# First weight matrix loaded in one transfer per quarter, its first tile swapped while converting, under a new order of all steps

## The chip, the core and the metric

The kernel runs on one core of one Trainium2 chip. The metric is the device time of one execution in microseconds (us), as the median of several executions; lower is better. A profile is one execution taken by the hardware profiler, with times counted from its first instruction. The engines are PE (matmuls; PEld is its loading of stationary operands), DVE, ACT and POOL (which convert, scale, mask and copy), and SP, which here only issues transfers. SPq is SP's queue of such issues.

## What is computed

Attention over 4 batches, 8 heads, 768 positions of width 64, then a two-layer network over the 3072 rows that come out of it. Heads 0, 2 and 6 are causal over all keys; in the other five each query sees the first four keys and the last 64. Inputs and output are 32-bit; the matmuls take bf16.

```
scores = q @ k^T / 8
keep   = causal                                    (heads 0, 2, 6)
         causal and (key < 4 or query - key < 64)  (other heads)
a      = softmax(scores where keep)
x      = (a @ v) with the heads side by side       [3072, 512]
h      = x @ w_in                                  [3072, 2048]
out    = (h / (1 + exp(-beta * h))) @ w_out        [3072, 512]
```


## The kernel before

**Units.** The work is cut into eight units n = 0..7: batch n // 2 and half n % 2 of its 768 positions, 384 rows each. A unit goes through these steps, named here by a letter, the unit and an index:

- loads of q, k (`load_qk` for units 0 to 2, four pairs of heads each; `load_block` for units 3 to 7, two blocks of three transfers) and of v (`load_v`), each followed by a conversion to bf16 (`cast_...`), mostly on POOL;
- T: transposes of q and k on PE (units 0 to 2); units 3 to 7 use a transposing transfer instead (`turn_block`, three per unit, written QK<-c in the profile);
- S: score matmuls, followed by E, the exponential on ACT, and M, the masks on DVE;
- sum: the row sums on PE. In units 0 and 1 their reciprocals stay on chip (rec and hl on DVE, sb on PE); from unit 2 on they go out and come back spread over the partitions by transfers (`sums_turn`, `spread_w`, `spread_r`, tile R);
- O: a @ v on PE, then the normalisation into xT, 512 x 384 in bf16;
- h.n.s for s = 0..15 (`mm1`, line 899): four matmuls that make 128 of the 2048 columns of h; then t.n.s (`swish_a`, ACT) and g.n.s (`swish_b`, DVE);
- m.n.1 to m.n.48 (`mm2`, line 916): the 48 matmuls of the second layer, 16 for each of three blocks of 128 rows; the sums are copied out (`out_copy`) and stored (`out_store`).

**Weights.** Both weight matrices are loaded once, in quarters, each into one of three staging buffers `wf` of 1 MB that the q, k and v blocks of later units also use (`RINGS`, line 217). A quarter of w_in covers 512 columns and four tiles of 128 rows. In the first tile the two halves of 64 rows must change places, because the pair of heads that makes the first 128 rows of xT lies the other way round (`XT`). `load_w_in` (line 472) does that while loading: one transfer of 768 KB for tiles 1 to 3 and two of 128 KB for the halves of tile 0. Then four conversions of 128 x 512 on POOL (`cast_w_in`, line 489) write `w_in_sb`. Quarter s serves h.n.4s to h.n.4s+3. A quarter of w_out is one transfer of 1 MB and four conversions; conversion i serves second-layer step i in each block of 16.

**The order.** Nothing is ordered by the loops. Every step is put in a list (`plan.add`) with its engine or a choice of engines, a price, what it needs and which buffers it takes. `SEQUENCE` (line 37) is a written-out permutation of that list and `CHOICE` (line 92) picks the engine where there is a choice. `_Plan.run` (line 137) goes through the list in that order, gives each step a start by the prices, and sorts by it; the code is then emitted in that order, and each engine runs its own steps strictly in the order of emission. So an engine whose next step must wait holds back everything behind it, SP's issues included. The prices are only used for that sorting, and for one more thing: in the first two units, wherever PE is planned to be idle before a step, `fill` (line 513) puts in matmuls with no use of their result, one per 0.14 us of planned gap.

**Transfers in flight.** The transfers use eight semaphores in turn, and an issue waits until the earlier transfer on its semaphore has landed, so that at most eight are in flight.

In every profile line the source line is that of a helper (L112 before), so groups are told apart by tile names.

Of the kernel before, what the change touches and what calls it, by code (L numbers as in the profile page):

```python
# [25 lines left out]
RD = 2  # L26
# [11 lines left out]
    474, 475, 6, 466, 4, 8, 14, 468, 12, 478, 467, 20, 10, 0, 2, 16, 5, 469, 473, 9, 7, 33, 471, 29, 77, 34,  # L38
    31, 13, 89, 32, 15, 30, 37, 477, 18, 50, 38, 39, 51, 11, 79, 40, 85, 1, 56, 43, 52, 3, 490, 35, 25, 41,
    27, 36, 26, 57, 42, 28, 17, 44, 45, 21, 47, 78, 91, 48, 53, 80, 97, 54, 59, 86, 102, 480, 23, 100, 24,  # L40
    101, 58, 103, 60, 49, 116, 19, 46, 117, 118, 55, 61, 22, 120, 62, 463, 121, 485, 479, 492, 119, 122, 73,
    493, 90, 63, 92, 491, 123, 114, 75, 64, 74, 81, 115, 112, 76, 83, 125, 481, 65, 87, 126, 67, 113, 69, 484,
    66, 134, 482, 71, 68, 135, 483, 137, 108, 70, 500, 139, 109, 72, 488, 520, 82, 93, 524, 138, 84, 104, 464,
    140, 127, 489, 95, 465, 528, 521, 494, 105, 522, 529, 486, 532, 536, 495, 136, 525, 487, 530, 106, 142,
    526, 88, 533, 143, 534, 502, 540, 107, 98, 110, 503, 547, 505, 111, 94, 541, 128, 548, 131, 501, 542, 551,
    132, 124, 555, 141, 129, 96, 549, 556, 559, 133, 159, 130, 560, 504, 557, 99, 144, 552, 510, 499, 553,
    155, 145, 497, 537, 498, 538, 157, 156, 496, 146, 515, 507, 563, 158, 509, 561, 570, 508, 564, 160, 147,
    523, 571, 148, 506, 527, 565, 572, 163, 531, 167, 153, 149, 151, 511, 535, 171, 150, 512, 161, 152, 574,
    513, 165, 154, 578, 575, 514, 173, 582, 579, 576, 169, 580, 586, 583, 218, 518, 592, 584, 476, 587, 517,
    596, 588, 516, 470, 597, 519, 539, 593, 598, 162, 543, 546, 594, 168, 222, 550, 172, 554, 174, 170, 184,  # L50
    185, 558, 544, 164, 166, 562, 190, 186, 188, 191, 193, 175, 189, 566, 187, 600, 221, 196, 569, 573, 192,
    601, 577, 194, 581, 567, 219, 181, 602, 198, 220, 604, 199, 197, 182, 224, 608, 201, 200, 585, 609, 195,
    227, 225, 203, 605, 610, 589, 223, 204, 606, 228, 612, 202, 206, 590, 205, 619, 613, 207, 226, 176, 208,
    620, 177, 623, 621, 209, 591, 614, 210, 627, 631, 229, 628, 635, 632, 629, 237, 633, 636, 235, 642, 568,
    624, 637, 239, 646, 238, 650, 211, 647, 625, 240, 212, 178, 472, 269, 595, 651, 648, 241, 599, 652, 242,
    654, 179, 643, 249, 655, 603, 236, 252, 644, 213, 658, 250, 253, 607, 656, 659, 244, 660, 611, 247, 271,
    615, 245, 618, 622, 243, 251, 616, 254, 248, 273, 626, 180, 255, 630, 257, 183, 634, 246, 256, 638, 258,
    272, 641, 639, 259, 270, 617, 645, 260, 649, 261, 214, 216, 231, 215, 280, 653, 232, 657, 217, 275, 661,
    664, 662, 274, 278, 668, 665, 276, 672, 669, 666, 277, 676, 262, 673, 230, 233, 670, 674, 677, 279, 678,
    680, 684, 681, 691, 682, 263, 685, 695, 326, 692, 686, 699, 693, 696, 703, 700, 697, 707, 663, 701, 714,  # L60
    704, 708, 718, 289, 705, 709, 715, 722, 726, 716, 264, 723, 234, 667, 727, 290, 281, 671, 724, 293, 282,
    728, 675, 719, 283, 291, 730, 720, 679, 731, 292, 315, 284, 295, 732, 683, 296, 687, 298, 690, 694, 688,
    300, 297, 698, 319, 303, 294, 327, 301, 302, 702, 304, 328, 706, 265, 299, 329, 267, 266, 689, 305, 330,
    545, 268, 710, 306, 713, 717, 307, 721, 370, 725, 317, 736, 729, 737, 321, 740, 738, 316, 711, 733, 324,
    741, 744, 318, 734, 748, 320, 742, 745, 752, 322, 749, 746, 323, 756, 308, 753, 750, 763, 754, 325, 757,
    767, 764, 758, 771, 640, 765, 768, 775, 309, 772, 366, 769, 779, 773, 776, 786, 777, 790, 787, 286, 780,
    788, 334, 332, 285, 739, 335, 287, 794, 336, 781, 743, 795, 310, 337, 791, 796, 747, 338, 792, 798, 339,
    369, 802, 799, 346, 367, 803, 800, 751, 349, 373, 368, 804, 755, 347, 376, 759, 762, 288, 760, 341, 372,
    766, 344, 333, 375, 770, 340, 342, 371, 774, 343, 374, 351, 350, 345, 778, 354, 348, 377, 782, 352, 785,
    311, 353, 355, 313, 312, 356, 789, 357, 314, 793, 358, 386, 797, 331, 387, 735, 801, 390, 712, 412, 808,  # L70
    388, 812, 809, 378, 392, 813, 810, 805, 395, 379, 814, 816, 391, 783, 359, 380, 820, 806, 817, 360, 824,
    416, 821, 818, 828, 822, 825, 835, 393, 826, 839, 396, 829, 836, 397, 830, 843, 389, 837, 840, 847, 361,
    844, 841, 851, 394, 848, 845, 415, 858, 849, 862, 852, 413, 859, 866, 853, 414, 860, 870, 863, 417, 864,
    400, 811, 419, 871, 815, 398, 418, 872, 422, 819, 867, 823, 868, 421, 399, 874, 401, 381, 827, 875, 420,
    402, 876, 362, 403, 404, 364, 363, 761, 831, 834, 423, 365, 838, 842, 429, 846, 880, 832, 850, 405, 881,
    431, 406, 882, 884, 807, 432, 382, 383, 888, 885, 892, 889, 886, 384, 854, 424, 890, 893, 857, 433, 861,
    426, 833, 855, 865, 407, 894, 869, 385, 896, 900, 425, 897, 434, 898, 907, 436, 911, 901, 784, 908, 873,
    902, 856, 877, 909, 912, 915, 878, 913, 919, 430, 916, 879, 427, 923, 920, 917, 930, 924, 921, 934, 435,
    925, 938, 931, 942, 932, 939, 408, 943, 940, 410, 409, 935, 883, 887, 411, 946, 944, 443, 936, 947, 891,
    895, 446, 447, 948, 952, 444, 953, 438, 954, 899, 441, 903, 439, 956, 442, 445, 906, 957, 448, 437, 958,  # L80
    910, 449, 914, 451, 450, 440, 918, 904, 960, 452, 453, 922, 454, 961, 926, 455, 964, 962, 968, 965, 905,
    929, 969, 933, 966, 937, 970, 428, 941, 945, 927, 949, 456, 972, 928, 950, 457, 979, 973, 983, 980, 974,
    987, 981, 984, 991, 988, 985, 995, 989, 992, 1002, 996, 993, 458, 1006, 997, 1003, 1010, 1007, 1004, 1014,
    1008, 1018, 1015, 955, 1011, 1016, 1012, 1019, 951, 1020, 959, 963, 967, 971, 975, 978, 976, 982, 977,
    986, 990, 994, 998, 1001, 999, 1005, 459, 460, 1000, 461, 1009, 462, 1013, 1017, 1021, 1024, 1022, 1028,
    1025, 1023, 1032, 1029, 1026, 1036, 1030, 1033, 1040, 1037, 1034, 1044, 1038, 1041, 1051, 1045, 1042,
    1055, 1046, 1052, 1059, 1056, 1053, 1063, 1057, 1060, 1067, 1064, 1061, 1073, 1065, 1068, 1076, 1069,
    1079, 1077, 1027, 1080, 1078, 1031, 1081, 1074, 1082, 1075, 1085, 1083, 1035, 1086, 1084, 1039, 1087,
    1043, 1047, 1048, 1050, 1054, 1049, 1058, 1062, 1066, 1070, 1088, 1071, 1089, 1072, 1092, 1090, 1091,
    1093, 1094, 1095,  # L90
]
CHOICE = (
    "aaddagaggdgdadadadaadddaddaaddgaagggdaaadaadaaaddaaaddaggdgdgaggadggdgdaadaadaaadaadadadddadddaaa"
# [95 lines left out]
def kernel(  # L189
# [15 lines left out]
    B, H, S, D = q.shape  # L205
    d_model, d_ff = moe_w_in.shape
    FO = d_ff // 128
    NP = len(PAIRS)
# [263 lines left out]
    def load_w_in(s):  # L472
        f = stg.tile([128, 2048], F32, name="wf", bufs=RINGS["wf"]).rearrange("p (a n) -> p a n", a=NP)

        def rows(r, n, tiles):
            return bass.AP(moe_w_in.tensor, moe_w_in.offset + r * d_ff + s * 2 * FS,
                           [[d_ff, n], [128 * d_ff, tiles], [1, 2 * FS]])
        sp.dma_start(out=f[:, 1:4, :], in_=rows(128, 128, 3))
        sp.dma_start(out=f[0:D, 0:1, :], in_=rows(D, D, 1))
        sp.dma_start(out=f[D:128, 0:1, :], in_=rows(0, D, 1))  # L480
        wst["i", s] = f
# [7 lines left out]
    def cast_w_in(s, i, eng):  # L489
        c = slice(i % 2 * 128, (i % 2 + 1) * 128)  # L490
        cast(eng, w_in_sb[2 * s + i // 2][:, :, c], wst["i", s][:, :, i * 128:(i + 1) * 128])
# [473 lines left out]
    def attention(n, early):  # L965
# [3 lines left out]
        for pi in range(NP if n < TD else 0):  # L969
            for nm in ("q2", "k2"):  # L970
                e = "act" if n == 0 and nm == "k2" else "sp"
                add(e, 0.47, lambda pi=pi, nm=nm, e=e: load_qk(x, pi, nm, ENG[e]), dma=0.63,
                    gives=[("f", n, pi, nm)], take=[(nm + "f", (n, pi), 1)])
                e = ("pool", "dve", "act") if early else ("pool",)
                add(e, [{"dve": 0.3, "pool": 0.47, "act": 0.41}[i] for i in e],
# [265 lines left out]
```

## Time and profile before

| | us |
|---|---|
| median of three executions | 240.97 (240.55 to 242.45) |
| span of the profiled execution, first to last instruction | 238.9 |
| median less span | 2.1 |
| PE busy, all stages | 224.3 |
| DVE busy / ACT busy / POOL busy | 153.9 / 141.9 / 90.8 |
| first h.0.s matmul starts | 27.98 |
| last matmul of the program ends | 235.8 |

The page cuts the span into 40 slices of 6 us and gives busy shares in tenths. For the stages the answer by windows is of more use: in it each row is a stretch (from:to, its length), then for PE, PEld, DVE, ACT and POOL the busy time and the number of instructions, then the TensorE clock that was granted (1.00 is full), the busy share of the 16 DMA engines (it can go a little over 1, since packets overlap) and GB/s. From 43 us to 235.8 us PE is busy 189.4 of 192.8 us by that answer; from 0 to 28 it is busy 22.1 and from 28 to 43 12.7.

A row of a group or of the timeline reads: line, engine, operation, output tile <- input tiles, shapes, count; a bracket gives the idle time before it and what ended that.

### The profile page before, as it was taken

The numbers are of one execution on the slowest core, as the hardware profiler recorded it, in microseconds if no ns is written. First come the engines' busy times: TensorE is split into PE (matmuls) and PEld (weight loads), VectorE is DVE, ScalarE is ACT, GpSimd is POOL, SyncE is SP. The second block draws the span as 40 slices with busy tenths as digits, with TensorE's granted clock in tenths as the row PEclk, the third lists the DMA queues.
The fourth block names the chain that finished last, engine by engine and source line by source line (L and its number), as shares of the span: only waits on it lengthen the run. The fifth ranks groups of instructions, "written<-read, shape, count | busy, mean of one in ns | idle before, by whom it ended". The sixth has DMA issues, their size and how long they took to land.

```text
span 238.9 us, 6057 instructions
## 1 busy us (share of the span) xinstructions
PE 224.3 (94%) x2359; PEld 128.6 (54%) x2385; DVE 153.9 (64%) x354; ACT 141.9 (59%) x238; POOL 90.8 (38%) x199
## 2 busy tenths in 40 slices
PE   8678996999999999999999999999999999999994
PEld 8535555555555456546544545564465555466553
DVE  4539869783968838865686548787475477157620
ACT  3858785456889518761679569707677437107611
POOL 7204759587632845696536173403600000000000
PEclk9956999999999999999999999999999999999999
DMA  6999699999989979999998999789910026211012
GB/s 197 273 307 321 205 258 354 300 314 211 175 196 240 211 162 189 214 230 223 225 231 179 169 230 231 149 178 216 219 71 3 0 92 150 80 44 47 0 44 88
DMA packets 92108, 43.14 MB, mean 181 GB/s; under 512 B 75936, under 2 KB 84848, under 8 KB 92080
## 3 DMA queue, kind: packets, MB, share of 16 engines
q1 hardware_dynamic: 90992, 41.98, 76.0%
q10 hardware_dynamic: 1088, 0.79, 1.1%
q8 instruction: 18, 0.29, 0.5%
q14 instruction: 10, 0.08, 0.1%
HBM read 32.38 MB, written 6.37 MB: 162 GB/s over the span
## 4 chain that ended last, share of the span: by engine, by line
PE 70%; DMA 9%; DVE 8%; SPq 4%; POOL 3%; ACT 3%; issue 2%; POOLq 0%
PE b L112 60%; PE sp L112 10%; SPq L112 4%; DMA QK<-c 3%; DMA wf<-in_v_dram 2%; POOL c L112 2%; DMA wf<-in_k_dram 2%; DMA q2f<-in_q_dram 2%; DVE es L112 2%; DVE gT L112 1%; ACT t L112 1%; DVE vs L112 1%; DVE QK L112 1%; ACT es L112 1%; DVE KP L112 1%
## 5 line engine op out<-in xcount | busy, mean ns | idle before, releaser
L112 ACT ACTIVATE t<-b,beta_h 128x384 f32<-128x384 f32 x128 | 72.4, 582 | 40.3 <-PE b L112 29.2
L112 DVE SCALAR_TENSOR_TENSOR gT<-t,b 128x384 bf16<-128x384 f32 x128 | 68.9, 551 | 37.1 <-ACT t L112 33.2
L112 PE MATMUL b<-xT,w_in 128*128 128x384 bf16 x512 | 90.3, 326 | 1.4 <-POOL w_in L112 0.9
L112 PE MATMUL b<-w_out,gT 128*128 128x512 bf16 (+1 forms) x374 | 87.1, 370 | 2.7 <-issue 1.8
L112 PEld LDWEIGHTS <-w_in 128*128 128x128 bf16 x512 | 49.0, 98 | 38.7 <-issue 2.6
L112 PEld LDWEIGHTS <-gT 128*128 128x128 bf16 x400 | 36.9, 98 | 38.7 <-issue 2.4
L112 ACT ACTIVATE es<-sp 128x768 bf16<-128x768 f32 (+3 forms) x64 | 49.1, 806 | 11.1 <-PE sp L112 10.7
L112 POOL CAST c<-wf 128x256 bf16<-128x256 f32 x60 | 23.2, 432 | 21.2 <-DMA wf<-in_q_dram 13.7
L112 PE MATMUL sp<-QK 64*64 64x64 bf16 (+6 forms) x402 | 19.9, 242 | 4.0 <-DVE QK L112 1.5
L112 ACT ACTIVATE osb<-b 128x512 f32<-128x512 f32 (+1 forms) x14 | 8.0, 568 | 23.9 <-PE b L112 16.9
L112 PEld LDWEIGHTS <-QK 64*64 64x64 bf16 (+1 forms) x402 | 10.4, 107 | 15.2 <-issue 12.1
L112 POOL COPY KP<-QK 128x64 bf16<-128x64 bf16 (+4 forms) x36 | 10.2, 332 | 21.6 <-DMA QK<-c 21.6
L112 POOL CAST w_in<-wf 128x512 bf16<-128x512 f32 x16 | 10.7, 699 | 15.2 <-DMA wf<-in_moe_w_in_dram 15.2
L112 POOL CAST vb<-wf 128x512 bf16<-128x512 f32 x18 | 12.2, 696 | 11.2 <-DMA wf<-in_v_dram 11.1
L112 DVE TENSOR_TENSOR es<-es,mask_c 128x256 bf16<-128x256 bf16 (+2 forms) x32 | 12.1, 394 | 4.2 <-ACT es L112 4.0
L112 DVE TENSOR_TENSOR es<-es,mask_s 128x800 bf16<-128x800 bf16 (+5 forms) x24 | 12.9, 551 | 2.7 <-ACT es L112 2.7
L112 DVE TENSOR_TENSOR xT<-sp,R 128x768 bf16<-128x768 f32 (+3 forms) x18 | 11.6, 687 | 4.0 <-PE sp L112 3.9
L112 DVE TENSOR_SCALAR osb<-b 128x512 f32<-128x512 f32 x11 | 7.5, 681 | 9.9 <-PE b L112 7.7
L112 PE MATMUL sp<-es,vb 128*64 128x64 bf16 (+3 forms) x243 | 13.8, 237 | 0.0
L112 POOL COPY vs<-vb 64x1536 bf16<-64x1536 bf16 (+2 forms) x9 | 12.2, 1361 | 2.5 <-issue 2.1
L112 PEld LDWEIGHTS <-vb 128*64 128x64 bf16 x243 | 11.8, 111 | 0.3
L112 POOL CAST w_out<-wf 128x512 bf16<-128x512 f32 x16 | 10.1, 667 | 2.2 <-DMA wf<-in_moe_w_out_dram 2.1
(91 smaller groups left out, 169.8 us busy)
## 6 DMA issues: line engine op xcount, KB each, us to landing
out_dram<-osb SPq DMA_DIRECT2D x23, 256.0 KB
wf<-in_v_dram SPq DMA_DIRECT2D x18, 256.0 KB
wf<-in_moe_w_out_dram SPq DMA_DIRECT2D x4, 1024.0 KB
wf<-in_q_dram SPq DMA_DIRECT2D x15, 256.0 KB
wf<-in_k_dram SPq DMA_DIRECT2D x15, 256.0 KB
R<-rd SPq DMA_DIRECT2D x9, 384.0 KB
wf<-in_moe_w_in_dram SPq DMA_DIRECT2D x4, 768.0 KB
q2f<-in_q_dram SPq DMA_DIRECT2D x12, 192.0 KB
```

What stands on the lines that cost most here:

```text
L112: ins = f(*a, **k)
```

## The change

1. `load_w_in` issues one transfer of 1 MB per quarter, in the order of the rows in memory.
2. `cast_w_in` converts tiles 1 to 3 only (128 x 384 instead of 128 x 512). A new step `swap_w_in` converts the first tile: two instructions of 64 x 256 per half quarter, each reading one half of the partitions and writing the other. Eight such steps (w0.0 to w0.7) exist; POOL, DVE or ACT may take each. `mm1` needs w0.(s // 2) besides the conversion of tiles 1 to 3, and a staging buffer of w_in is now released by six steps instead of four.
3. Several prices are changed (among them: w_in quarter 3.5 to 2.9 us of transfer, R 6.2 to 3.8, sums 0.85 to 1.7).
4. `SEQUENCE` and `CHOICE` are new, 1104 steps instead of 1096.

```
     def load_w_in(s):
         f = stg.tile([128, 2048], F32, name="wf", bufs=RINGS["wf"]).rearrange("p (a n) -> p a n", a=NP)
-        def rows(r, n, tiles):
-            return bass.AP(moe_w_in.tensor, moe_w_in.offset + r * d_ff + s * 2 * FS,
-                           [[d_ff, n], [128 * d_ff, tiles], [1, 2 * FS]])
-        sp.dma_start(out=f[:, 1:4, :], in_=rows(128, 128, 3))
-        sp.dma_start(out=f[0:D, 0:1, :], in_=rows(D, D, 1))
-        sp.dma_start(out=f[D:128, 0:1, :], in_=rows(0, D, 1))
+        sp.dma_start(out=f, in_=bass.AP(moe_w_in.tensor, moe_w_in.offset + s * 2 * FS,
+                                        [[d_ff, 128], [128 * d_ff, NP], [1, 2 * FS]]))
         wst["i", s] = f
...
-        cast(eng, w_in_sb[2 * s + i // 2][:, :, c], wst["i", s][:, :, i * 128:(i + 1) * 128])
+        cast(eng, w_in_sb[2 * s + i // 2][:, 1:, c], wst["i", s][:, 1:, i * 128:(i + 1) * 128])
+
+    def swap_w_in(s, half, eng):
+        f = wst["i", s][:, 0, half * FS:(half + 1) * FS]
+        for r in (0, D):
+            cast(eng, w_in_sb[2 * s + half][r:r + D, 0, :], f[D - r:2 * D - r, :])
...
-        add("pe", 0.65, lambda: mm1(x, s), needs=[("xT", n, t) for t in range(NP)] + [("wi", s)] +
+        add("pe", 0.65, lambda: mm1(x, s), needs=[("xT", n, t) for t in range(NP)] + [("wi", s), ("w0", s // FO2)] +
...
-            add("sp", 1.3 if w == "i" else 0.65, lambda s=s, ld=ld: ld(s), dma=3.5, gives=[("wf", w, s)], begun=[("begun", w, s)],
-                take=[("wf", (w, s), 4)])
+            add("sp", 0.5, lambda s=s, ld=ld: ld(s), dma=2.9, gives=[("wf", w, s)], begun=[("begun", w, s)],
+                take=[("wf", (w, s), 6 if w == "i" else 4)])
...
+            for half in range(2 if w == "i" else 0):
+                add(("pool", "dve", "act"), (0.7, 0.4, 0.7), lambda e, s=s, half=half: swap_w_in(s, half, ENG[e]), port=True,
+                    needs=[("wf", w, s)], gives=[("w0", 2 * s + half)], drop=[("wf", (w, s))])
```

What the new lists come to, read from the two programs as they are emitted (in.s and out.s are the quarters of w_in and w_out; q20 is q of unit 2, pair 0):

```
SP, from the loads of v.0 to the transposing transfers of unit 3
before: q01 q02 q03 v.0.2 q00 v.0.0 q10 q13 v.0.1 k10 q12 in.1 k13 v.1.2 in.0 beta out.0 q11 k11 k12 in.2 v.1.0 v.1.1
        out.1 out.2 q20 in.3 out.3 q21 q22 q23 k20 k21 k23 k22 unit3.q unit3.k v.2 edges QK.3 (3)
after:  q00 q01 q02 q10 q03 k10 beta q11 k13 q13 q12 v.0.0 v.0.1 v.0.2 in.1 in.0 k12 k11 in.2 v.1.0 in.3 v.1.2 v.1.1
        out.1 q20 k20 q21 out.0 out.3 out.2 k21 q22 k23 k22 q23 unit3.q unit3.k unit4.q edge QK.3 (3)
SP, from there to the transposing transfers of unit 4
before: store sum.2 v.3 store rd.2 unit4.q R.2 unit4.k store sum.3 v.4 QK.4 (3)
after:  v.2 sum.2 v.3 edge store rd.2 unit4.k R.2 store QK.4 (1) store v.4 sum.3 QK.4 (2)
PE, from the start of the second layer of unit 0
before: ... h.0.0-9 ... O.1 h.0.10-11 sb.1 m.0.1-12 h.0.12-15 h.1.0-1 m.0.13-24 T.2.0 m.0.25-30 T.2.3 T.2.1 T.2.2 S.2 m.0.32
        h.1.2 m.0.33-42 S.2 h.1.3-4 m.0.43-45 S.2 m.0.46-48 h.1.5-6 sum.2 h.1.7-10 S.3 ... O.2 m.1.40-48 h.2.0-14 m.2.1-3 S.4
after:  ... h.0.0-11 sum.1 O.1 h.0.12 T.2.0 sb.1 h.0.13-14 S.2 h.0.15 h.1.0-7 m.0.1-6 T.2.1 T.2.2 m.0.7-12 T.2.3 m.0.13-16
        h.1.8-10 S.2 h.1.11-13 m.0.17-24 h.1.14 S.2 h.1.15 m.0.25-32 m.1.1-6 sum.2 m.1.7-9 S.3 ... O.2 m.1.46-48 h.2.0-9 S.4
```

The eight swaps are placed on ACT (w0.1, 2, 3, 4, 6), POOL (w0.0, 7) and DVE (w0.5). In the program after, POOL's list has `wo.8 wo.10 wo.11 c.2.1.k2 c.2.2.q2 c.2.2.k2 wo.9`, that is, the conversions for T.2.1 and T.2.2 stand among those of quarter 2 of w_out, and DVE's list has w0.5 between two masks of unit 1 before g.0.0. The filling matmuls on constants number 84 before and 58 after.

## The prediction

> **What bounds the kernel now.** First the page: PE is nearly full, and the chain that ended last is mostly PE. So a gain must come from PE's empty or slow time, and a loss is a new wait of PE.
>
> ```profile
> PE 224.3 (94%) x2359; PEld 128.6 (54%) x2385; DVE 153.9 (64%) x354; ACT 141.9 (59%) x238; POOL 90.8 (38%) x199
> ...
> PEclk9956999999999999999999999999999999999999
> DMA  6999699999989979999998999789910026211012
> ...
> PE 70%; DMA 9%; DVE 8%; SPq 4%; POOL 3%; ACT 3%; issue 2%; POOLq 0%
> ...
> L112 PE MATMUL b<-xT,w_in 128*128 128x384 bf16 x512 | 90.3, 326 | 1.4 <-POOL w_in L112 0.9
> L112 PE MATMUL b<-w_out,gT 128*128 128x512 bf16 (+1 forms) x374 | 87.1, 370 | 2.7 <-issue 1.8
> ```
>
> The last two rows price PE's work: a step h is four matmuls, 90.3 / 128 = 0.70 us; a step m is 87.1 / 374 = 0.23. The DMA row says that transfers are busy for the first 29 slices, so the second limit is supply. The lost PE time lies early; by windows:
>
> ```profile
> 5.34:8.75 3.41, 2.77 (x50) 2.31 (x48) 0.82 (x3) 2.66 (x6) 1.01 (x2) 1.00 1.16 288
> 8.75:12.17 3.42, 1.96 (x29) 1.35 (x28) 2.71 (x8) 2.65 (x6) 1.18 (x2) 1.00 1.21 264
> 12.17:15.58 3.41, 2.50 (x29) 1.46 (x29) 0.63 (x2) 1.84 (x3) 0.00 (x0) 0.50 1.09 357
> ...
> 36.00:39.40 3.40, 1.66 (x20) 0.98 (x22) 3.40 (x7) 2.10 (x5) 3.01 (x6) 1.00 0.99 348
> ```
>
> PE idles, drops to half clock from 12.17 us (restored at 22.40), and waits once more for DVE at 36 to 39 us, where DVE is busy all 3.40. After 43 us it loses only 3.4 us up to its end. Then the holes of the supply, in the first and the third batch of loads:
>
> ```profile
> 26.00:27.00 1.00, 0.77 (x14) 0.46 (x13) 0.97 (x3) 0.40 (x2) 1.00 (x3) 1.00 0.39 118
> 27.00:28.00 1.00, 1.00 (x14) 0.49 (x11) 1.00 (x3) 0.86 (x2) 0.90 (x3) 1.00 0.07 22
> 28.00:29.00 1.00, 1.00 (x9) 0.61 (x8) 0.65 (x3) 1.00 (x3) 1.00 (x3) 1.00 0.42 153
> ```
>
> ```profile
> 87.00:88.00 1.00, 1.00 (x6) 0.46 (x5) 1.00 (x2) 0.00 (x0) 0.96 (x3) 1.00 0.16 39
> 88.00:89.00 1.00, 1.00 (x7) 0.52 (x6) 0.02 (x1) 0.17 (x1) 1.00 (x4) 1.00 0.20 46
> ```
>
> DMA is short by 0.61 + 0.93 + 0.58 = 2.1 us in the one and 0.84 + 0.80 = 1.6 us in the other. SP's rows show the first cause: after the two k2f it waits until 27.33, when quarter 0 of w_in has been converted and gives its buffer back.
>
> ```profile
> 20.50 1.39 SPq L112 DMA_DIRECT2D k2f<-in_k_dram  x2
> 27.33 1.55 SPq L112 DMA_DIRECT2D wf<-in_moe_w_in_dram  x3
> ```
>
> Two rows of POOL date what PE will need: quarter 0 of w_in has landed at 25.01, and the transposes of unit 4 at 97.72, where POOL's copy had waited 4.95 us for them.
>
> ```profile
> 25.01 2.29 POOL L112 CAST w_in<-wf 128x512 bf16<-128x512 f32 x4 [2.94 <-DMA wf<-in_moe_w_in_dram]
> ```
>
> ```profile
> 97.72 2.12 POOL L112 COPY KP<-QK 128x300 bf16<-128x300 bf16 x7 [4.95 <-DMA QK<-c]
> ```
>
> **The loads and the swap.** SP loses eight of twelve issues of w_in; at 1.55 / 3 = 0.52 us each that is 4 us of its queue, and eight turns among the eight transfers in flight. It is worth nothing by itself: the bytes are the same, and the semaphore counts in the trace show quarter 1 landing at 18.56 (768 KB), 19.12 and 19.45 us (128 KB each), so the halves cost only their bytes. The Trainium skill ("DMA: Bandwidth & Descriptors", section "Anatomy of one DMA") gives a fixed cost of about 2 us to each DMA on the software path; eight of these would be 16 us, and 225 us the time. The rows do not show it, and I take none of it.
>
> Conversion: POOL's 128 x 512 takes 0.70 us (10.7 / 16 = 0.67 by busy time), 128 x 384 of k2f 0.51, so 16 x 0.16 to 0.19 = 2.6 to 3.0 us less on POOL. The swap adds 16 instructions of 64 x 256, not in the trace. POOL: bounds 0.31 (128 x 64 copy) and 0.51, I take 0.43 (128 x 256), 4 x 0.43 = 1.7. ACT: 0.38 (128 x 256 out of PSUM) to 0.51, I take 0.40, 10 x 0.40 = 4.0. DVE: 0.25 to 0.36, 2 x 0.3 = 0.6. POOL is not the bound there (38%); ACT is close to it from 7 to 43 us, and the five swaps on it stand ahead of O.0's copies, E.1.3.1 and t.0.2 and t.0.10, on which O.0, S.1.3 and h.0 wait. They are in the walk below.
>
> **The new order up to 43 us.** Fix the state of before at 43.1 us: h.0.0 to 9, all of O.1, and PE full from there. In the order after, when h.0.15 has ended, PE has done beyond that six h (4.2), four sb (0.25 each by 2.0 / 8), T.2.0 (0.5): 5.7 us of work.
>
> When is that? h.0.0 needs quarter 0 of w_in. With it 14 transfers of q and k (0.197 MB each), three of v (0.262) and two quarters (1.049) have landed in the new order, 5.6 MB; before it was the end of 5.7 MB. So it lands at 25.0 as before, or, if the supply keeps the pace of its best stretches, near 22.5. POOL then does two conversions, c.1.1.k2, the swap w0.0 and two conversions: 4 x 0.51 + 0.51 + 0.86 = 3.4, so h.0.0 is at 26.0 to 28.4; before it was 27.98. From there to the end of h.0.15 PE has 16 h (11.2), S.1.3.3 and S.1.2.0 (0.9), sum.1 (1.5), O.1 (2.46), sb (1.0) and T.2.0 (0.5) = 17.6 us. DVE has from the first t onwards 16 g at 0.54 (8.6), two masks (1.3), vs.1 (1.25), v.1.2 (0.4), reciprocal and split (2.25), xT (2.0) = 15.8 us: it fits beside PE but barely. At PE's busy share before from 28 to 43 us, 12.7 / 15 = 0.85, it would be 20.7 us, at full 17.6; I take 18.5. From 27.2 that ends at 45.7. Lead: 5.7 - (45.7 - 43.1) = 3.1 us; ends 27.2 + 20.7 gives 0.9, 26.0 + 17.6 gives 5.2.
>
> **Unit 2.** The T steps of unit 2 follow when six m of unit 0 are done, and wait for k21 and k22, which now stand behind all four quarters of w_out; POOL converts them among quarter 2 of w_out. All loads of unit 2 end at 54.4 in the trace's semaphore counts. The same bytes at that pace bring k22 one load of 0.65 us earlier, T.2.3 is done at 56.7; with the first hole filled (2.1 us) at 54.6. Then m.0.13 to 32 (0.9 + 3.7) and the state of before at 58.17 (h.1.2 begins) is reached at 61.3 or 59.2, with six more h done (4.2): lead 1.1 or 3.2 us. Filled is the nearer: quarter 2 of w_in finds a free buffer, since the new order has two quarters in front of it and not three.
>
> **Unit 4.** Before, S.4 started at 99.08. In the order after five h (3.5) and three m (0.7) fewer stand before it, so with a lead L it comes at 94.9 - L. It needs QK.4. From the start to QK.4 the list of transfers is the same in both, only turned round. So at the old pace QK.4 lands at 97.7, and PE waits: L = -2.8. With the first hole filled 95.6 (L = -0.7), with both 94.0 (L = 0.9). Below that: q of unit 4 is converted long before, so the three transposes are not held up by POOL as they were (6.12 us of SP for three, 1.28 each: 2.3 us), at most 91.7 (L = 3.2). SP's own new wait here: the store of unit 1 waits for a copy on DVE, whose list stands behind reciprocal 2, and v.4 is queued behind that store; R.2 covers it. I take 93.4, L = 1.5; from unit 5 on the new list has QK.n ahead of more loads than before, and the order of before met them without waits over 0.5 us, so I cost the rest at nothing; what hides it is DMA at 0.70 busy after 70 us, and without that cover it costs what QK.5 cost, 0.48.
>
> **Clock.** The half rate from 12.17 came although PE was 69% busy in the 6.83 us before (2.77 + 1.96) and never idle for more than 1.11 us. With 26 filling matmuls fewer (84 to 58) it will come again, and may last longer. One more window of 3.41 us at half rate costs up to 1.7 us of PE. I take 0, since up to h.0.0 ACT's exponentials and the load of quarter 0 set the pace; both ends stay in the range. The Trainium skill ("TensorE: Matmul & The Clock Gate", section "Why this matters for your kernels") asks for no idle gaps over about 3 us to keep the rate; by that rule the fewer fillers cost nothing, but the rows above, with no such gap and yet half rate, speak against it.
>
> **Sum.** Of the three gates the lowest counts: 3.1, 2.1 (middle), 1.5. So 238.9 - 1.5 = 237.4 of span, plus 2.1 around it: 239.5 us.
>
> **Rivals.**
> - Slower: supply keeps the old pace up to QK.4, because the swaps on ACT and DVE give the w_in buffers back late and SP stalls as it did before. For it: w0.6 stands behind t.0.9, w0.5 between masks. Against it: three buffers are free at the start. Price: L = -2.8, 243.8 us. It decides from QK.4 landing after 94.9 us.
> - Much faster: both holes go and QK.4 lands at 91.7: L = 3.1 to 4, 237.0 to 238 us. For it: eight issues fewer and SP's waits gone; against it: the lowest of three gates must be high in all.
> - No change because unit 2 eats it: T.2 waits at the old pace, and half clock lasts a window longer: 1.1 - 1.7 = -0.6, 241.6 us.
>
> **How the numbers follow.** A measurement of this kernel tells about 1%, 2.4 us. Forecast (gains of 0.5 to 2.6) 0.44, at 239.5, own range 238.4 to 240.5; much faster 0.24; no change 0.16; slower 0.16. Faster by over 1% (below 238.6) is the second and a tenth of the first: 0.28. Slower by over 1% (above 243.4) is most of the last and some of waits that I did not see in a wholly new order: 0.18. Same: 0.54. The range leaves out the ends of the faster and the slower case: 236.5 to 243.8.
>
> **What would show it.** h.0.0 at 26 to 28.4 and h.0.15 ended by 46.5; no DMA share below 0.5 from 20 to 50 us; T.2.3 done by 55; POOL's copy KP of unit 4 starting by 94 with S.4 right behind; the half clock over by 26. It is wrong if PE shows a wait of over 1 us on QK<-c or on c (unit 2), if DMA holes return between 20 and 100 us, or if stalls come after unit 4.

## The result and the profile after

| | before | after |
|---|---|---|
| median (executions) | 240.76 (4) | 237.74 (4) |
| lowest to highest | 240.38 to 242.45 | 237.50 to 239.24 |
| span of the profiled execution | 238.9 | 236.2 |
| first h.0.0 / end of h.0.15 | 27.98 / 50.58 | 27.39 / 45.20 |
| last of QK.4 landed / S.4 starts | 97.5 / 99.08 | 93.12 / 93.26 |
| last matmul ends | 235.79 | 232.97 |

The ratio to the time before is 0.9879, 95% interval 0.9832 to 0.9925. Every ratio here compares executions that lie within 1.5% of the fastest of their kernel. The same kernel was run once more beside later experiments ("control"): 237.70, ratio 0.9835 (0.9800 to 0.9869). So the change makes the kernel faster, by 1.2% and by 1.7% in the two measurements.

The page of after, the lines that answer to those of before:

```profile
PE 224.1 (95%) x2337; PEld 128.3 (54%) x2359; DVE 148.9 (63%) x340; ACT 145.3 (62%) x247; POOL 94.1 (40%) x220
...
PEclk9965999999999999999999999999999999999999
DMA  6989999999999999999959899975570025210312
...
PE 72%; DMA 18%; POOL 3%; SPq 2%; issue 2%; DVE 1%; ACT 0%; DVEq 0%; ACTq 0%
```

PE is as busy as before, in a span 2.7 us shorter: what went is time in which PE stood. The half clock is there again, as long as before (10.24 us). In the chain DMA now has 18% where it had 9, and DVE 1 where it had 8: the transfers became the second part of the path, behind PE. Next the answer by windows of after, at the two holes of the supply, and at the lowest share from 20 to 50 us (at 32) and from 50 to 100 us (at 97):

```profile
27.00:28.00 1.00, 0.90 (x16) 0.61 (x17) 0.01 (x1) 1.00 (x3) 0.04 (x1) 1.00 1.05 364
28.00:29.00 1.00, 1.00 (x8) 0.59 (x6) 0.96 (x4) 0.98 (x3) 0.63 (x1) 1.00 1.05 378
32.00:33.00 1.00, 1.00 (x9) 0.60 (x7) 0.58 (x2) 1.00 (x4) 0.95 (x3) 1.00 0.52 124
87.00:88.00 1.00, 1.00 (x9) 0.59 (x7) 0.99 (x3) 0.88 (x2) 0.00 (x0) 1.00 1.39 218
88.00:89.00 1.00, 1.00 (x8) 0.61 (x7) 0.81 (x3) 0.90 (x3) 0.00 (x0) 1.00 1.35 210
97.00:98.00 1.00, 1.00 (x42) 0.55 (x43) 0.54 (x1) 0.20 (x1) 0.58 (x2) 1.00 0.29 63
```

The last two columns are the DMA share and GB/s: both holes are filled (0.07 to 1.05 at 27 us, 0.16 to 1.39 at 87). PE's largest wait is the one before S.4, in the timeline of PE (start, length, then what ran and, in brackets, the idle time before it):

```profile
88.80 3.25 PE L113 MATMUL b<-xT,w_in 128*128 128x384 bf16 x19
93.26 0.50 PE L113 MATMUL sp<-QK 64*128 64x384 bf16 x6 [1.20 <-DMA QK<-c]
```

SP's timeline shows why QK.4 comes no sooner. Its first part is issued at 80.60, the other two only behind a store, the loads of v.4 and the spreading of sum.3:

```profile
80.60 1.31 SPq L113 DMA_TRANSPOSE QK<-c  x1
81.96 0.57 SPq L113 DMA_DIRECT2D out_dram<-osb  x1
82.59 3.44 SPq L113 DMA_DIRECT2D wf<-in_v_dram  x3
86.13 1.74 SPq L113 DMA_DIRECT2D rec<-sc  x2
87.98 2.65 SPq L113 DMA_TRANSPOSE QK<-c  x2
```

### The profile page after: what moved, and what is told of

The parts are those of the page before. It is cut to its first block, busy times and chain, and to the rows that moved or that the text cites. A ratio compares the mean times of both kernels' runs of the same rounds, so it can differ in the third digit from the quotient of the medians.

```text
span 236.2 us, 5989 instructions
## 1 busy us (share of the span) xinstructions
PE 224.1 (95%) x2337; PEld 128.3 (54%) x2359; DVE 148.9 (63%) x340; ACT 145.3 (62%) x247; POOL 94.1 (40%) x220
## 4 chain that ended last, share of the span: by engine, by line
PE 72%; DMA 18%; POOL 3%; SPq 2%; issue 2%; DVE 1%; ACT 0%; DVEq 0%; ACTq 0%
PE b L113 63%; PE sp L113 9%; DMA wf<-in_moe_w_out_dram 7%; DMA vf<-in_v_dram 7%; DMA q2f<-in_q_dram 2%; SPq L113 2%; DMA QK<-c 2%; POOL w_out L113 1%; POOL c L113 1%; DVE xT L113 1%; DVE c L113 0%; POOL vb L113 0%; ACT t L113 0%; DVE mask_s L113 0%; ACT osb L113 0%
## 5 line engine op out<-in xcount | busy, mean ns | idle before, releaser
L113 PE MATMUL b<-xT,w_in 128*128 128x384 bf16 x512 | 91.6, 326 | 0.9 <-DVE gT L113 0.6
L113 PEld LDWEIGHTS <-gT 128*128 128x128 bf16 x400 | 37.6, 98 | 39.2 <-issue 1.9
L113 ACT ACTIVATE osb<-b 128x512 f32<-128x512 f32 (+1 forms) x17 | 9.9, 585 | 25.9 <-PE b L113 20.0
L113 POOL COPY KP<-QK 128x64 bf16<-128x64 bf16 (+5 forms) x47 | 12.8, 320 | 27.8 <-DMA QK<-c 25.7
L113 POOL CAST vb<-wf 128x512 bf16<-128x512 f32 x18 | 11.6, 667 | 16.2 <-DMA wf<-in_v_dram 16.2
L113 PE MATMUL sp<-es,vb 128*64 128x64 bf16 (+3 forms) x243 | 14.7, 245 | 0.0
L113 DVE TENSOR_TENSOR es<-es,mask_c 128x256 bf16<-128x256 bf16 (+2 forms) x32 | 10.7, 348 | 2.7 <-ACT es L113 2.4
L113 POOL CAST w_in<-wf 128x384 bf16<-128x384 f32 (+1 forms) x20 | 10.1, 537 | 5.7 <-DMA wf<-in_moe_w_in_dram 5.4
L113 ACT COPY QK<-b 128x384 bf16<-128x384 bf16 (+1 forms) x16 | 8.3, 548 | 5.0 <-PE b L113 2.8
```

The costliest lines, as they stand in the source:

```text
L113: ins = f(*a, **k)
```

## The experiments

**Loads and order apart.** Two kernels put the old part into the new and the new into the old. `new_order_old_loads` is the changed kernel with

```
-        sp.dma_start(out=f, in_=...)
+        sp.dma_start(out=f[:, 1:4, :], in_=rows(128, 128, 3))
+        sp.dma_start(out=f[0:D, 0:1, :], in_=rows(D, D, 1))
+        sp.dma_start(out=f[D:128, 0:1, :], in_=rows(0, D, 1))
...
-        cast(eng, w_in_sb[...][:, 1:, c], wst["i", s][:, 1:, ...])
+        cast(eng, w_in_sb[...][:, :, c], wst["i", s][:, :, ...])
...
     def swap_w_in(s, half, eng):
-        ...
+        pass
```

> The changed kernel with the old loads of w_in: three transfers for a quarter, conversions of 128x512 on POOL, no swaps (the eight swap steps do nothing). Theory (the order alone makes the gain, the merged loads are worth nothing by themselves): span 236.2 within 0.6, QK.4 landed at 93.1 and S.4 right behind it, the first h.0 at 27.4. Rival (the eight issues saved on SP carry part of the gain): eight issues of 0.52 us come back into SP's queue ahead of QK.4, so QK.4 lands up to 4 us later, S.4 starts at 95 to 97 and the span is 238 to 240. Second rival (the swaps cost more than the issues save): faster than the changed kernel, 235 or less, with h.0.0 ahead of 27.0.

`old_order_new_loads` is the kernel before with the new load and conversion, and behind conversions 0 and 2 of each quarter:

```
+        if i % 2 == 0:
+            half = i // 2
+            f = wst["i", s][:, 0, half * FS:(half + 1) * FS]
+            e = {0: pool, 7: pool, 5: dve}.get(2 * s + half, act)
+            for r in (0, D):
+                cast(e, w_in_sb[2 * s + half][r:r + D, 0, :], f[D - r:2 * D - r, :])
```

> The kernel before, in its old order, with one transfer for a quarter of w_in, conversions of 128x384 and the swaps (two instructions of 64x256 behind the first and the third conversion of a quarter, on the engines that the change gives them). Theory: 238.9 within 0.6, S.4 at 99.1, the DMA hole at 27 us still there, since SP still waits for the buffer of quarter 0. Rival (the loads carry the gain): 237.3 or less, QK.4 landed by 96. Rival (swaps cost): over 239.6, with PE waiting for the swaps before h.0.

| ratio to the time before | old loads | new loads |
|---|---|---|
| old order | 1 | 1.0047 (1.0006 to 1.0088) |
| new order | 1.0002 (0.9973 to 1.0031) | 0.9879, again 0.9835 |

Neither part gains anything alone. The new loads in the old order are even slightly slower (six of the twelve executions enter this ratio; the profiled one, 244.34 us, does not and is not read here). Its list has no steps for the swaps, which simply follow the conversions, so what the new loads are worth in an old order planned around them is left open. The new order with the old loads has a span of 240.3 us, S.4 at 97.36, 4.1 us later than after. The theory that the order alone makes the gain has fallen, and so has the rival that the loads do. Where the new order loses with the old loads is in PE's waits (engine, what it waited for: total, times, longest):

```profile
PE b L113 <- POOL c L113: 5.4, 3, 4.0
PE sp L113 <- DMA QK<-c: 1.6, 1, 1.6
```

One wait of 4.0 us, for POOL's conversion of k11, which T.1.1.1 needs. POOL's timeline, first after:

```profile
20.12 1.66 POOL L113 CAST w_in<-wf 128x384 bf16<-128x384 f32 x3 [2.78 <-DMA wf<-in_moe_w_in_dram]
22.86 0.96 POOL L113 CAST w_in<-wf 128x384 bf16<-128x384 f32 x2 [1.08 <-DMA wf<-in_moe_w_in_dram]
24.04 0.51 POOL L113 CAST c<-k2f 128x384 bf16<-128x384 f32 x1 [0.21 <-DMA k2f<-in_k_dram]
```

and in the new order with the old loads:

```profile
21.92 1.73 POOL L113 CAST w_in<-wf 128x512 bf16<-128x512 f32 x3 [4.52 <-DMA wf<-in_moe_w_in_dram]
25.46 1.17 POOL L113 CAST w_in<-wf 128x512 bf16<-128x512 f32 x2 [1.82 <-DMA wf<-in_moe_w_in_dram]
27.63 0.51 POOL L113 CAST c<-k2f 128x384 bf16<-128x384 f32 x1 [0.99 <-DMA k2f<-in_k_dram]
```

The two quarters that the new order has in front (the waits for `wf`) and then k11 come 1.8, 2.6 and 3.6 us later. By the semaphore counts, the second of two quarters loaded back to back lands 2.74 us after the first in one transfer each (20.07 to 22.81; 2.71 in the control), and 3.55 us after it in three (21.77 to 25.32).

A part of the loss comes behind h.0.0. It starts 2.66 us later than after (30.05), and h.0.15 ends 4.04 us later (49.24). Behind PE's wait the clock was halved from 27.64 to 34.47 us. In all four profiles of the new order with three transfers a half clock lies over the first h steps; in the eight others of the new order none does, and that stretch ends by 24.5 us. The total does not rest on this alone: among executions with a mean clock of 0.977 to 0.979 the seven of this kernel have spans of 238.1 to 241.0 us, the six of after and control 235.5 to 237.5.

**Transfers or conversions.** `three_transfers` keeps the new conversions and swaps and splits only the load, without turning the halves:

```
-        sp.dma_start(out=f, in_=...)
+        sp.dma_start(out=f[:, 1:4, :], in_=rows(128, 128, 3))
+        sp.dma_start(out=f[0:D, 0:1, :], in_=rows(0, D, 1))
+        sp.dma_start(out=f[D:128, 0:1, :], in_=rows(D, D, 1))
```

> The changed kernel, its conversions and swaps kept, with a quarter of w_in loaded in three transfers again (768 KB and two of 128 KB of 64 rows each, the rows of the first tile in their own order). It parts the two halves of the earlier run with old loads. Theory (the transfers: two quarters in six pieces land 1.7 and 2.5 us later than in two, and k12 and k11 behind them 3.6 us later, and POOL's conversion for T.1.1.1 stands behind both quarters): quarter 1 lands at 21.8 and quarter 0 at 25.3, PE waits 3.5 to 4.5 us at 24 us, S.4 at 97, span 240.0 to 240.8. Rival (the conversions of 128x512 on POOL in place of 128x384 and the swaps were what cost): as the changed kernel, 235.5 to 236.8.

Measured: 0.9997 (0.9965 to 1.0029), span 240.1, S.4 at 97.1, the second quarter 4.0 us behind the first (21.79 to 25.80). So the transfers are the cause, and neither the width of POOL's conversions nor the swaps. The single wait at 24 us that I had expected is split here (0.84 us at 23.5, 1.22 at 26.2); its place was not right, the loss was.

The traces also show what the split does to the supply. From 22 to 24 us, first after and then in the new order with the old loads:

```profile
22.00:24.00 2.00, 2.00 (x33) 1.41 (x29) 1.35 (x5) 1.79 (x4) 0.96 (x2) 0.68 1.07 368
22.00:24.00 2.00, 1.67 (x19) 0.87 (x19) 1.50 (x4) 1.42 (x3) 1.65 (x3) 1.00 1.08 275
```

The DMA engines are equally busy (1.07 and 1.08) and move 368 and 275 GB/s. Packets of 2 KB, of which the quarters are made, take 91 ns on average from 20 to 28 us after, and 109 to 120 ns in the four runs with three transfers. So the bytes are the same and the packets are slower. In those four runs SP also waits 2.8 to 4.1 us between 8 and 30 us until pieces of w_in have landed; after it has no such wait. Why a packet gets slower, and whether the number of transfers counts or the 64 rows of the two small ones, was not tested.

**What waits for the late quarters.** Two kernels with the old loads move k12 and k11 in front. Moves of this kind are made in the sorted list, without changing any other step:

```
-        return [x[2:] for x in sorted(order, key=lambda x: x[:2])]
+        order = sorted(order, key=lambda x: x[:2])
+        for behind, ids in MOVES:
+            moved = [x for i in ids for x in order if x[1] == i]
+            order = [x for x in order if x[1] not in ids]
+            at = [x[1] for x in order].index(behind) + 1
+            order[at:at] = moved
+        return [x[2:] for x in order]
```

`old_loads_k_first`: behind the load of k11, the loads of in.1 and in.0.

```
+        MOVES = [(83, [492, 480])]
```

> The new order with the old loads of w_in and no swaps, as in the earlier run, but with the loads of k12 and k11 ahead of the first two quarters of w_in on SP instead of behind them. Theory (the old loads cost the new order its gain only because six issues of 0.6 us then stand ahead of k12 and k11, on which T.1.2.1 and T.1.1.1 wait): PE's wait of 3.97 us at 24 us falls to under 1, h.0.0 starts by 28, and the span is within 0.8 of the changed kernel's 236.2. Rival (the issues themselves, or 128 KB transfers, cost the whole chain behind them): span 239 or more although k12 and k11 come early.

`k_first_both`: there too POOL's conversion of k11.

```
+        MOVES = [(83, [492, 480, 84])]
```

> The new order with old loads and no swaps, k12 and k11 ahead of the first two quarters of w_in on SP, as in the earlier run, and now POOL's conversion of k11 too, ahead of its first conversion of w_in. Theory (in the earlier run k11 had landed at 17.6 us and was converted at 27.9, since POOL stood waiting for the two quarters in front of it): PE's wait of 4.4 us at 24 us shrinks to what quarter 0 costs; with quarter 0 landed at 26.7 and four conversions of 0.6 behind it, h.0.0 starts at 29.3, S.4 at 95.3, and the span is 238.1 to 238.9, half of the loss. Rival (T.1.1.1 is not what the rest waits for, quarter 0 is): h.0.0 at 30.3 and the span over 240 as before.

Both expectations of a gain failed: 1.0044 (1.0011 to 1.0077), span 240.7, and 1.0003 (0.9968 to 1.0037), span 241.7. In the first, k11 had landed at 17.6 and POOL still converted it at 27.9, behind both quarters. In the second it did so at 18.0:

```profile
18.03 0.51 POOL L113 CAST c<-k2f 128x384 bf16<-128x384 f32 x1 [0.49 <-DMA k2f<-in_k_dram]
24.10 1.73 POOL L113 CAST w_in<-wf 128x512 bf16<-128x512 f32 x3 [5.56 <-DMA wf<-in_moe_w_in_dram]
28.41 3.52 POOL L113 CAST w_in<-wf 128x512 bf16<-128x512 f32 x6 [2.58 <-DMA wf<-in_moe_w_in_dram]
```

and PE then stood for quarter 0 itself, before h.0.0, which started at 30.87:

```profile
PE b L113 <- POOL w_in L113: 3.4, 1, 3.4
```

So the late quarters hold PE at two places, T.1.1.1 and h.0.0, and taking away one shows the other. With k12 and k11 ahead of it quarter 0 itself also lands later, at 26.70 and 28.30 us after 25.32. In the kernel after both quarters land sooner, which helps at both places.

**QK.4 earlier.** `qk4_first` moves the two later parts of QK.4 ahead of store, v.4 and sum.3:

```
+        MOVES = [(275, [277, 278]), (261, [648, 280])]
```

> The changed kernel with the last two transposing transfers of unit 4 ahead of the store, the loads of v of unit 4 and the spreading of the sums of unit 3 on SP; before they stood behind them. Theory (QK.4 is the last gate, and PE is full behind it): QK.4 lands near 89, PE's wait of 1.20 us before S.4 goes, S.4 starts at 92.0, and the span falls by 1.2 to 235.0. Rival (PE's wait there is cover for other work that is late anyway, so a wait of the same size comes next, on R.3, on v.4 or on QK.5): S.4 at 92.0 and the span at 236 or above, with a new wait over 0.5 us after 95 us.

Measured: 1.0038 (1.0007 to 1.0069), slower, though QK.4 landed at 87.6. The store had been moved as well, and PE's waits show the price:

```profile
PE b L113 <- DVE osb L113: 3.7, 1, 3.7
```

and DVE's timeline what that copy waited for:

```profile
89.87 0.69 DVE L113 TENSOR_SCALAR osb<-b 128x512 f32<-128x512 f32 x1 [4.84 <-DMA out_dram<-osb]
```

The store was issued at 87.64 (81.96 after), the copy waited for the buffer that it gives back, and PE, which needs the bank of PSUM that this copy gives back, stood for 3.74 us from 86.87. `qk4_store_kept` leaves the store in place:

```
+        MOVES = [(275, [277, 278]), (261, [280])]
```

> The changed kernel with the last two transposing transfers of unit 4 ahead of the loads of v of unit 4 and of the spreading of the sums of unit 3, the store staying where it was (in the earlier run the store was moved too, a copy on DVE waited for its buffer, and PE stood 3.74 us for that copy). Theory (QK.4 holds S.4, and only that): QK.4 lands by 90, S.4 follows the tenth h of unit 2 without a wait at 92.0, span 1.2 less than the control's. Rival (SP's list behind is as tight, so v.4 or the sums of unit 3 come late instead): the wait before S.4 goes, and the same 0.6 to 1.2 us come back as waits between 100 and 130 us; span within 0.4 of the control's.

Measured: 236.85 us, 0.9806 (0.9770 to 0.9843), beside the control's 237.70 and 0.9835. The intervals overlap, so the times alone do not part the two. The profiles show a wait gone and a part of it back. PE's timeline at S.4, and then at S.5:

```profile
92.27 0.50 PE L113 MATMUL sp<-QK 64*128 64x384 bf16 x6
...
111.08 0.50 PE L113 MATMUL sp<-QK 64*128 64x384 bf16 x4 [0.40 <-DMA QK<-c]
```

S.4 starts 1.30 us earlier than in the control, without a wait; QK.5 then costs 0.40, and the last matmul ends 0.57 earlier (232.72 against 233.28). This lies between theory and rival: the wait before S.4 is real, and in these two profiles less than half of it is to be had.

`qk4_and_k12_first` adds that ACT converts k12 ahead of its swap w0.1:

```
+        MOVES = [(275, [277, 278]), (261, [280]), (66, [88])]
```

> The kernel with the last two transfers of unit 4 ahead of v of unit 4 and of the sums of unit 3, and in addition ACT's conversion of k12 ahead of its swap w0.1, behind which it stood (PE waits 0.9 us for it at 25.4 us). Theory (a lead at the start of h passes through to the end once QK.4 is not waited for): PE's wait at 25 us falls to 0.1, h.0.0 starts 0.2 to 0.5 us earlier, bound then by POOL's conversions of quarter 0, and the span is 235.4 to 235.7 against 235.9. Rival (the time is held by later waits, QK.5 and the copies on DVE): 235.9 or more.

Measured: 237.06 us, 0.9823 (0.9788 to 0.9858), span 236.1: no gain that shows. The wait at 25 us went, but this execution waited longer elsewhere before it (1.48 us at 7.2, for a conversion on DVE) and h.0.0 came at 28.39, so the lead at h was not tried.

**The control, and PE's work on either side of the sums.**

> The changed kernel as it is, run beside the other three. Theory and rival alike: 0.988 of the time before, QK.4 landed at 93.1 and PE's wait of about 1.2 us before S.4 again. If the stretch of half clock comes at another time or for another length than 13.0 to 23.3 us, S.4 should still start within 0.5 us of 93.3 by the theory that QK.4 sets it, and up to 2 us earlier or later by the rival that PE's own pace does.

Its QK.4 landed at 93.43 and the wait was 1.56 us. `work_before_s4` and `work_behind_sum2` do two h steps twice:

```
-        for pi in range(NP):
+        for pi in list(range(NP)) * (2 if (x.n, fi) in ((1, 3), (1, 4)) else 1):
```

with (2, 3), (2, 4) in the second.

> The changed kernel with the four matmuls of h.1.3 and of h.1.4 done twice: 1.4 us more work for PE at 47 us (2 x 0.70), between the second gate and S.4. Theory (QK.4, a matter of SP's queue and the transfers, holds S.4 and not PE): 1.20 us of it goes into the wait before S.4, which starts at 93.3 to 93.5, and the span grows by 0 to 0.3. Rival (PE bounds all the way, QK.4 comes when PE's steps let it): S.4 at 94.6 and the span at 237.6, with the wait before S.4 still there.

> The changed kernel with the four matmuls of h.2.3 and of h.2.4 done twice: 1.3 us more work for PE at 87 us, between the sums of unit 2 and S.4. Theory (SP's list from the sums of unit 2 onwards is a chain of its own; QK.4 lands 25 to 26 us after the copy of those sums whatever PE does in between, which makes the wait of 1.2 to 1.6 us before S.4, and extra work ahead of the sums delays both, as the earlier run with work at 47 us showed): the wait before S.4 shrinks to 0 to 0.3, S.4 starts at 93.3 to 93.6, the span is 236.2 to 236.8. Rival (PE bounds there too): S.4 at 94.6 or later, span 237.5 to 238.

Measured: 0.9927 (0.9895 to 0.9959), span 237.0, and 0.9951 (0.9922 to 0.9980), span 237.9. In the second, S.4 started only 0.40 us later than in the control (93.97 after 93.57) for 1.3 us of work, as the theory of QK.4 has it. The wait before it shrank to 0.83 only and not to 0.3 or less, since QK.4 too landed 0.40 later. But the end came 1.44 later. Of the missing 1.0, 0.68 was lost around O.3, where PE waits 0.46 and 0.22 us for DVE and not at all in the control; the rest was not traced. The timeline of both engines, in the control (whose line numbers are higher by one):

```profile
103.41 1.56 POOL L114 CAST vb<-wf 128x512 bf16<-128x512 f32 x2
104.53 0.92 DVE L114 COPY vs<-vb 4x1344 bf16<-4x1344 bf16 x1
105.04 1.50 POOL L114 COPY vs<-vb 64x1536 bf16<-64x1536 bf16 x1
```

and with the work behind the sums:

```profile
104.91 1.68 POOL L113 COPY vs<-vb 64x1536 bf16<-64x1536 bf16 x1
105.30 1.77 DVE L113 COPY vs<-vb 4x1344 bf16<-4x1344 bf16 x1
```

DVE's small copy, 0.8 us late, now begins after POOL's copy instead of before it. In both runs it ends 0.48 us past the end of the POOL instruction that was running when it began. In the control that is a conversion, which ends at 104.97 (103.41 + 1.56), and the copy takes 0.92 us; with the work behind the sums it is POOL's copy, which ends at 106.59 (104.91 + 1.68), and the copy takes 1.77. PE waits for it. Where POOL is idle the same copy takes 0.62 us (`qk4_first`, at 109.16). In `work_before_s4` the same copy took 1.77 as well; there the early stage ran 1.0 us ahead of the control's, the half clock lasted 3.4 us only, and S.4 came at 93.07. So that run leaves open what its 1.4 us cost by themselves.

**The clock.** `more_fillers`:

```
-        for _ in range(int(held["gap"] / 0.14)):
+        held["fills"] = held.get("fills", 0) + 1
+        for _ in range(int(held["gap"] / (0.14 if held["fills"] < 4 else 0.05))):
```

> The changed kernel with a filling matmul for each 0.05 us of planned gap instead of 0.14, from the third place of filling on: some 65 more between 7 and 29 us. Theory (the clock falls when a window of 3.41 us holds too little PE work, and the pace up to h.0.0 is set by the exponentials and by quarter 0 of w_in): the half clock is shorter than 10.2 us, h.0.15 ends up to 1 us earlier, and the span falls by 0 to 1 us, since QK.4 holds S.4. Rival (the fillers only push real work back): the half clock comes as before, h.0.0 after 28, span 236.5 to 238.

Measured: 0.9999 (0.9955 to 1.0044), span 241.0, with 39 more filling matmuls and not 65. Each of the two was right in one thing only: the half clock fell to one stretch of 3.41 us, as the theory has it, and nothing was gained, as the rival has it. h.0.0 came at 27.84 and the span lies above both forecasts: h.0.15 ended 1.1 us later than in the control, S.4 came 2.7 later and the end 4.5 later, with 1.88 us of wait before S.4 and 1.24 at O.3. Why 1.1 us grew to 4.5 was not taken apart.

## Why the prediction was right, and where it was not

**The early walk held.** h.0.0 at 27.39 (27.2 taken), h.0.15 ended at 45.20 (45.7), T.2.3 done at 54.51 (54.6 or 56.7), QK.4 landed at 93.12 (93.4), S.4's lead 94.9 - 93.26 = 1.64 (1.5). No DMA share from 20 to 50 us was below 0.52, KP of unit 4 started at 93.33, the half clock was over at 23.27. Of the signs against it one came: PE waits 1.20 us on QK<-c. Single DMA shares of 0.49 at 61 us and 0.29 at 97 were left, where PE was busy throughout.

**The step that failed: "It is worth nothing by itself: the bytes are the same".** In the old order that is so. In the new order the merged loads are the whole gain. I had read the landings of one quarter's pieces (0.56 and 0.33 us apart) and not asked what two quarters in a row do to what is queued behind them: 2.7 us a quarter in one transfer, 3.4 to 4.4 in three, over the four runs with three. The Trainium skill ("DMA: Bandwidth & Descriptors", section "Anatomy of one DMA") gives about 2 us fixed to a DMA on its software path; the runs show 0.3 to 0.8 us for each transfer added on SP's queue, far less, but not the nothing that I took. The bytes are the same, and what I had not priced is the rate at which they come (from 22 to 24 us 368 GB/s with one transfer, 275 with three, at the same DMA share). The forecast came out because it dated quarter 0 from the old landing (25.0) and the best pace (22.5); it landed at 22.81, and with three transfers at 25.32 to 28.30. By my own reckoning the new order with the old loads would have gained about as much, and it gained nothing: as to the loads, the number came out by luck.

**Gate 3 had the right date for the wrong reason.** I dated QK.4 by the bytes in front of it. The runs show it tied to the sums of unit 2: SP issues their spreading when PE's sum has been copied out, and the last of QK.4 lands 24.7 to 26.4 us later in eight of the nine profiles that keep SP's list from there (after: 67.87 to 93.12; old loads: 71.40 to 97.22; 27.7 with more fillers), while that start itself moves by 5 us (67.3 to 72.3). So the gates are not three separate bounds of which the lowest counts: a late early stage moves the third along, at full price. With the old loads h.0.15 ended 4.0 us later, and S.4 and the end came 4.1 later.

**"I cost the rest at nothing"** was 1.2 us short: 2.82 us of lead at the last matmul against 1.64 at S.4. QK.5's wait (0.48) went. A run of h steps shows 0.667 us for one (38 matmuls in 6.34 us), not 0.70, which is 0.2 of it over the 5 h. The remaining 0.5 was not traced.

**What lies around the span** was 2.1 us by the median less a span of another execution. After, each execution's time less its own span is 1.7; that is 0.4 of the 1.8 by which 239.5 is too high; 1.2 are the rest, 0.14 is S.4.

**The clock at 0** was right. Three of the executions of before beside the control were granted full clock all the way: 241.94, 242.31 and 239.86 us, among others of 240.1 to 243.2.

**The rivals.** Slower, "supply keeps the old pace": its mechanism is real (QK.4 at 97.2 with the old loads), its cause was not the swaps, and the merged loads kept it away. No change: T.2.3 came by 54.51 and no window was added. Much faster: the time lies in its 237 to 238, but its condition (QK.4 at 91.7) was not met. I gave most to a gain too small to tell from none; it was just above that.

## What to carry to other kernels

A split transfer is not priced by its bytes. Here merging gained nothing in one order of the steps, and decided over the whole gain in another, where two such transfers in a row stand ahead of critical loads: look at the GB/s at full DMA share, at what is next on the issuing queue, and at the converting engine that stands behind. Test two parts of one change in all four combinations before saying which one gains. Before a step is moved ahead of another on a queue, ask what that other one gives back: here a store issued 5.7 us later stopped PE for 3.7.

## What was not expected of the hardware

- The half clock comes in pieces of 3.41 us, and the same program does not get the same ones. The kernel after had it for 10.24 us from 13.03; `work_before_s4`, identical up to 47 us, for 3.41. Before and after it came with no PE gap above 1.2 us ahead of it; in other runs it came after long waits of PE: 3.74 us in `qk4_first` (one piece, 91.4 to 94.8) and 3.97 us in `new_order_old_loads` (two, 27.64 to 34.47). The Trainium skill ("TensorE: Matmul & The Clock Gate", section "Why this matters for your kernels") asks for no gaps over about 3 us; that fits the long waits and not the early stage.
- A copy on DVE (4 x 1344) that begins while POOL has an instruction running ends 0.48 us past the end of that instruction: it took 0.92 us behind the last 0.44 of a conversion, 1.77 behind 1.29 of a copy, and 0.62 beside an idle POOL. The Trainium skill ("SBUF — State Buffer", section "Who interferes with whom") says of a DVE instruction in a two-port mode and one on POOL that the second to issue is blocked until the first is done; the ends agree, though no run here shows the mode.
- Matmul records are missing from some profiles: 374 and 378 of 400 of the second layer are on the pages of before and after. The gaps of 0.16 us ahead of such steps, marked as waits for "issue", are not there in the runs where all 400 are, so they are more likely the place of a missing record than idle time.
